# Turning the normed rows on VectorE and carrying the blocks with 32-partition copies, in a Fourier-mixing and feed-forward kernel

## The chip, the cores and the metric

The kernel runs on one core of a Trainium2 chip. The metric is device time in microseconds (us) of one execution: the median of several runs. Next to it stands one execution recorded by the hardware profiler. Engines are named as the profile names them: PE (TensorE; PEld is its weight load), DVE (VectorE), ACT (ScalarE), POOL (GpSimd), SP (SyncE). "L1195" is line 1195 of the kernel before.

## The reference, cut to what matters

```python
q_s = softmax(q, axis=-1); k_s = softmax(k, axis=2)      # B, H, S, DH = 8, 8, 576, 64
x   = q_s @ (k_s.T @ v)                                  # to (B, S, 512)
mixed = real(fft(fft(x, axis=1), axis=2))
u   = x + mixed
un  = (u - mean(u)) / sqrt(var(u) + 1e-6)
out = u + maximum(un @ w_ch1, 0.0) @ w_ch2               # 512 x 2048, 2048 x 512
```

All is computed in float32.

## The kernel before, in words

The 8 x 576 = 4608 rows of u are handled in nine groups of 512 rows: groups 0 to 7 hold 512 rows of one batch each, and group 8 the rows left over from all batches ("shared"). They are taken in the order 0, 1, ..., 6, 8, 7. Each group of four 128-row tiles passes an up stage (un times w_ch1, then relu) and a down stage (times w_ch2, plus u). Tile i has column half c = i % 2 of the group and row half u = i // 2. From the second group on, the up stage is a Strassen scheme of seven products (`ORDER = (1, 6, 5, 7, 2, 4, 3)`) in each of four pairs, L1334; from the third on, the down stage ("deep down") first runs product 1 (L1431), then three units of two products each, (2, 4), (7, 6) and (5, 3), in which the same scheme is applied once more (L1461).

While one group passes its stages, the next batch is prepared beside it: attention (with exponentials on ACT, L774 among them), the folded Fourier transform (`folded`, then `block`, L1087 and L1090, five of them, then `mix_own` and `mix_shared`, L1115 on), and the norm of the next group. `norm` takes the statistics of u (DVE, L1165), the root and scales (ACT L1169, DVE L1172), the normed tile un (ACT, L1189), turns it with four PE transposes of 128x128 into a PSUM tile (L1195), and copies that to the group's tile `unT` (ACT, L1204). `unT` is 128 x 7 x 2 x 256: seven slots, of which 0 to 3 hold the four quarters of un transposed and 4, 5, 1 and 6 get differences of quarters (`combine`: DVE and POOL, L1210; `combine_last`, L1215). The up stage's first products need slots 0, 5, 4 and 1, in this order. There is one buffer for `unT`, and the deep down stage of the group before uses its slots 0 to 5 as scratch in its unit (2, 4) only.

The order of work on each engine is written out by hand. Every step has a time in units ("steps") and an action; all steps are sorted by time, and each engine executes its instructions in that order, waiting at the head of its queue where data are late. In the deep down stage one unit is one product of eight matmul records on PE; the stage starts at 0, unit (2, 4) at 8, (7, 6) at 22, (5, 3) at 36, and the next up stage starts at 50. In a unit that starts at t the seven products start at t, t+2, ..., t+12. Their results are accumulated in three PSUM banks: ba (products 1 and 2), bb (6, 7, 4) and bc (5, 3). Between them other engines read the banks (`ends`): ACT copies ba after product 1 (L1475, at t+1.5) and after 2 (L1482, t+9.5); DVE reads bb after 6 (L1468, t+3.5) and after 7 (t+7.5, with one read of bc), bb after 4 (t+11.5) and bc after 3 (t+13.5). The next product into a bank waits for the read before it. On DVE and POOL there are also `a_step` (L1407: sums of blocks for the next unit; for (5, 3) at 25.3 to 32.4), and on POOL `into` and `sums` (L1411, L1414; additions to u and between blocks; from group 8's pass on both are done by DVE).

`norm` stands at step 29 of the down stage: statistics from 29.7, root 36.2, scales 38, normed tiles 38.3 to 42.2, transposes 40.8 to 44.7, copies 41.6 to 45.5, `combine` 46.5, `combine_last` 56.5. The norm of group 7 stands at step 14 of group 8's pass. In the first Strassen pass (group 1, "order 1"; its down stage has 56 steps without deep units, L1550) it stands at 29 too.

Of the kernel before, what the change touches and what calls it, by code (L numbers as in the profile page):

```python
# [40 lines left out]
F32 = mybir.dt.float32  # L41
# [5 lines left out]
P = 128  # L47
B, H, S, DH = 8, 8, 576, 64
D = H * DH
# [3 lines left out]
HD = D // 2  # L53
# [5 lines left out]
Q = 32  # L59
W = 2 * Q  # L60
NT = Q // 2 + 1
KT = D // P
VD = 4 * NC - S // Q
NF = FF // P
GT = 4 * P
NP = NF // 2

# [14 lines left out]
UP, TWICE = NP * len(ORDER), 8 + 6 * len(ORDER)  # L82
PAIRS = [(j + NP // 2, j) for j in range(NP // 2)]

DOWN = [(i, f) for n in range(4) for i in (2, 3, 0) for f in range(4 * n, 4 * n + 4)] + [(1, f) for f in range(NF)]
WARM = (3, 3), (24.7, 6), (41.9, 2), (43.45, 1), (44.5, 1)
# [32 lines left out]
def at(t, script):  # L119
    return [(t + dt, step) for dt, step in script]  # L120
# [17 lines left out]
class _Block:  # L138
    def __init__(self, ctx, tc, q, kT, v, w1, w2, ft, cd, out):
# [63 lines left out]

        self.big = c.tile([P, 3 * NF * D], F32, name="big")
        self.fifth = self.big[:, 3 * NF * D - 5 * P:3 * NF * D - P].rearrange("p (r n) -> p r n", n=P)
        nc.gpsimd.memset(self.fifth[0:64], 0.0)
        part = lambda i: self.big[:, i * NF * D:(i + 1) * NF * D].rearrange("p (f n) -> p f n", n=D)
        self.w1sb, self.w2sb, self.h0 = part(0), part(1), part(2)
# [15 lines left out]
    def turned(self):  # L224
        t = self.ps.tile([P, 4, P], F32, tag="tr", name="tr", bufs=2)
        return t
# [20 lines left out]
    def loads_first(self, fetch):  # L247

        nc, b = self.nc, 0
        at = 2 * NF * D  # L250

# [390 lines left out]
    def values_to(self, b, h):  # L642

        def load(i):
            first = VD * (i == 3)
            a = min(i * NC, S // Q - NC) + first
            v = self.v[b, :, h * HD:(h + 1) * HD].rearrange("(c s) n -> s c n", s=Q)[:, a:a + NC - first]
            self.nc.sync.dma_start(self.vt[i * Q:i * Q + Q, first:, 1:1 + HD], v)
# [3 lines left out]
    def prepare(self):  # L652
# [6 lines left out]
        for col in (0, 2 * P + 1):  # L659
            G.memset(self.vt[:, :, col:col + 1], 1.0)  # L660
        G.memset(self.vt[3 * Q:, 0:VD, :], 0.0)

# [493 lines left out]
    def norm(self, g):  # L1156

        nc, V = self.nc, self.nc.vector
        mv = self.small.tile([P, 4, 2], F32, tag="mv", name="mv", bufs=2)
        std = self.small.tile([P, 4], F32, tag="std", name="std", bufs=2)  # L1160
        uns, box = {}, {}

        def stats(i):
            st = self.small.tile([P, 6], F32, tag="st", name="st", bufs=2)
            V.bn_stats(st[:], self.xpart(g, i % 2, i // 2))  # L1165
            V.bn_aggr(mv[:, i, :], st[:])

        def root(s):
            nc.scalar.activation(std[:, s], mv[:, s, 1], ACT.Sqrt, bias=self.eps[:, 0:1])  # L1169

        def scales(s):
            V.reciprocal(std[:, s], std[:, s])  # L1172
            V.scalar_tensor_tensor(out=mv[:, s, 0], in0=mv[:, s, 0], scalar=-1.0, in1=std[:, s], op0=ALU.mult,
                                   op1=ALU.mult)

        def back():
            if g > 0:

                t = self.small.tile([P, 1], F32, tag="root", name="root", bufs=1)
                nc.scalar.activation(t[:], std[:, 0:1], ACT.Exp, scale=0.0)  # L1180

        def normal(i):
            un = self.halves()
            x = self.xpart(g, i % 2, i // 2)
            if g == 0 and i < 2:
                V.tensor_scalar(out=un[:, 0:D], in0=x, scalar1=std[:, i:i + 1], scalar2=mv[:, i, 0:1], op0=ALU.mult,
                                op1=ALU.add)
            else:
                nc.scalar.activation(un[:, 0:D], x, ACT.Identity, bias=mv[:, i, 0:1], scale=std[:, i:i + 1])  # L1189
            uns[i] = un  # L1190

        def turn(i):
            pt = self.turned()
            for k in range(KT):
                nc.tensor.transpose(pt[:, k, :], uns[i][:, k * P:(k + 1) * P], self.ident[:])  # L1195
            box[i] = pt

        def laid(i):
            if g not in self.unT:
                self.unT[g] = self.work.tile([P, 7, 2, HD], F32, tag="unT", name="unT", bufs=1)  # L1200
            c, u = i % 2, i // 2
            cols = slice(c * P, (c + 1) * P)
            copy = V.tensor_copy if g == 0 and c == u else nc.scalar.copy
            copy(self.unT[g][:, u:u + 3:2, :, cols], box.pop(i)[:].rearrange("p (a k) t -> p a k t", a=2))  # L1204

        def combine():
            if g > 0:
                some = lambda i: self.unT[g][:, i]
                for e, to, x, y in ((V, 4, 1, 0), (nc.gpsimd, 1, 3, 1), (V, 5, 3, 4)):
                    e.tensor_tensor(out=some(to), in0=some(x), in1=some(y), op=ALU.subtract)  # L1210

        def combine_last():
            if g > 0:
                some = lambda i: self.unT[g][:, i]
                V.tensor_tensor(out=some(6), in0=some(2), in1=some(5), op=ALU.subtract)  # L1215

        steps = []
        put = lambda t, f, *a: steps.append((t, lambda: f(*a)))
        if g == 0:
            for some in ((0, 2), (1, 3)):  # L1220
                s = slice(some[0], 4, 2)
                for i in some:
                    put(0, stats, i)
                for f in (root, scales):
                    put(0, f, s)
        else:
            for n, i in enumerate((0, 2, 1, 3)):
                put((0.7, 2.7, 4.7, 6)[n], stats, i)
            s = slice(0, 4)
            put(7.2, root, s)  # L1230
            put(9, scales, s)
            put(13.6, back)
        for n, i in enumerate((0, 2, 1, 3)):
            put(9.3 + 1.3 * n, normal, i)
            put(11.8 + 1.3 * n, turn, i)
            put(12.6 + 1.3 * n, laid, i)
        put(17.5, combine)
        put(27.5, combine_last)
        return steps
# [384 lines left out]
def kernel(ctx: ExitStack, tc: tile.TileContext, q, kT, v, w1, w2, ft,  # L1624
                                                           cd, out):
    blk = _Block(ctx, tc, q, kT, v, w1, w2, ft, cd, out)

    def timed(t, order, g):
        b = order + 1
        steps = at(t, blk.up(order, g)) + at(t + UP, blk.down(g, order))  # L1630
        if order == B:
            return steps + [(t + 6 + 1.2 * i, lambda i=i: blk.later and blk.later.pop(0)()) for i in range(36)]
        if b == B:
            return steps + at(t + UP + 14, blk.norm(groups[b]))
        start, end = -7 if order > 2 else 0, 45
        if b + 1 < B:
            steps += at(t, blk.ahead(b + 1))
        steps += at(t, blk.attention_timed(b, start, end)) + at(t + end, blk.folded(b))
        t += UP
        for i, k in enumerate((2, 3, 0, 1, 4)):  # L1640
            steps += at(t + 2 + 2 * i, blk.block(b, k))
        mixes = [blk.mix_own(b, c) for c in range(2)]
        if b % 2:
            mixes.insert(0 if b == B - 1 else 2, blk.mix_shared(b // 2))
        for i, some in enumerate(mixes):
            steps += at(t + 12.5 + 3.2 * i, some)
        return steps + at(t + 29, blk.norm(groups[b]))

    fetch, convert = blk.weights()

# [26 lines left out]
    groups = [*range(B - 1), B, B - 1]  # L1677
    first, second, both = 46.9, 56, 77
    steps = blk.opening(fetch, converted)
# [3 lines left out]
    t = first + second  # L1683
# [28 lines left out]
    t = 0  # L1712
    for order, g in enumerate(groups[1:], 1):
        later += timed(t, order, g)
        t += UP + (TWICE if order > 1 else UP)
# [59 lines left out]
```

## Time and profile before

| | |
|---|---|
| median of 3 runs | 1049.63 us (1049.01 to 1050.84) |
| profiled execution, its own time | 1050.86 us |
| its span, first to last instruction | 1049.1 us |
| PE clock granted | 0.998 |
| PE busy | 1034.9 us (99%) |
| DVE, ACT, POOL busy | 719.7, 456.3, 406.0 us |
| DMA | 236 MB, 225 GB/s on average |

Busy times are sums over one execution. PE's matmuls are pipelined, so their records overlap, and what a matmul costs is read from the starts of neighbours. The `unT` of group 2 is made at about 280 us, of groups 3, 4, 5, 6 and 8 at about 400, 511, 623, 734 and 847 us, and of group 7 at about 928 us (starts of the transposes).

### The profile page before, as it was taken

To read this page: it belongs to the slowest core of one execution; us is meant where nothing else is said; L and a number is where in the kernel's file an instruction comes from. 1 tells how busy PE (TensorE), PEld (TensorE's weight loads), DVE (VectorE), ACT (ScalarE), POOL (GpSimd) and SP (SyncE) were. 2 spreads that over 40 slices of the span, in tenths; PEclk is the share of its full clock that TensorE was granted. 3 is DMA by queue.
4 is the path that set the end of the run, shared out by engine and by line. 5 is a ranking of instruction groups with operands and counts; after the bars stand their busy time and mean duration, and the time that the engine had idled before them with its cause. 6 is when DMAs were issued, how large, how long until landed. Compare 5 with 4: busy or idle time off the path is not lost.

```text
span 1049.1 us, 16781 instructions
## 1 busy us (share of the span) xinstructions
PE 1034.9 (99%) x6178; PEld 901.0 (86%) x6178; DVE 719.7 (69%) x1410; ACT 456.3 (43%) x1141; POOL 406.0 (39%) x350
## 2 busy tenths in 40 slices
PE   8999999999999999999999999999999999999998
PEld 7844554888888899889998999989998998999898
DVE  5898888775476866777675777587658644774563
ACT  5674532862239216841475237822682132131210
POOL 3164420366333744555536544474346440000000
PEclk9999999999999999999999999999999999999999
DMA  8887598587999666955786567747644664576464
GB/s 254 258 266 257 172 255 285 185 243 231 290 321 231 214 219 245 238 201 193 259 225 201 201 241 242 217 176 256 228 154 178 224 241 161 216 255 221 171 224 147
DMA packets 114313, 236.01 MB, mean 225 GB/s; under 512 B 23272, under 2 KB 78696, under 8 KB 103608
## 3 DMA queue, kind: packets, MB, share of 16 engines
q1 hardware_dynamic: 113864, 234.42, 68.3%
q8 instruction: 49, 0.80, 0.3%
q14 instruction: 32, 0.26, 0.1%
q10 hardware_dynamic: 288, 0.26, 0.1%
q0 software_dynamic: 80, 0.26, 0.1%
HBM read 199.79 MB, written 39.06 MB: 228 GB/s over the span
## 4 chain that ended last, share of the span: by engine, by line
PE 81%; DVE 5%; DMA 3%; ACT 1%; issue 0%; POOL 0%; SPq 0%; DVEq 0%; ACTq 0%
PE bb L1334 15%; PE ba L1334 10%; PE bb L1461 10%; PE bc L1334 10%; PE bc L1461 7%; PE ba L1461 7%; PE bb L1431 5%; PE acc L715 2%; PE bb L1550 2%; PE acc L790 2%; DMA big<-w1s 2%; PE acc L1087 1%; PE acc L1090 1%; PE bc L1550 1%; PE ba L1550 1%; PE tr L1195 1%
## 5 line engine op out<-in xcount | busy, mean ns | idle before, releaser
L1334 PE MATMUL bb<-unT,big 128*128 128x256 f32 x768 | 182.0, 379 | 0.0
L1334 PEld LDWEIGHTS bb<-unT,big 128*128 128x128 f32 x768 | 144.3, 190 | 19.4 <-DVE u L1304 0.5
L1346 ACT ACTIVATE big<-big 128x512 f32<-128x512 f32 x96 | 60.3, 629 | 156.7 <-DVE big L1345 155.8
L1334 PE MATMUL ba<-unT,big 128*128 128x256 f32 x512 | 124.1, 379 | 1.1 <-DMA big<-w1s 1.1
L774 ACT ACTIVATE qT<-q 32x128 f32<-32x128 f32 x384 | 117.9, 307 | 13.9 <-DVE q L764 8.9
L1334 PE MATMUL bc<-unT,big 128*128 128x256 f32 x512 | 121.7, 379 | 0.0
L1334 PEld LDWEIGHTS bc<-unT,big 128*128 128x128 f32 x512 | 96.1, 190 | 13.2 <-DVE big L1345 0.7
L1334 PEld LDWEIGHTS ba<-unT,big 128*128 128x128 f32 x512 | 94.5, 190 | 13.3 <-DMA big<-w1s 1.3
L1461 PE MATMUL bb<-big 128*128 128x128 f32 x848 | 105.1, 275 | 0.3 <-DVE u L1468 0.3
L1304 DVE TENSOR_TENSOR u<-bb,s 128x512 f32<-128x512 f32 x66 | 45.4, 689 | 86.0 <-PE bb L1334 71.5
L1461 PEld LDWEIGHTS bb<-big 128*128 128x128 f32 x848 | 99.6, 192 | 0.5 <-DVE u L1468 0.5
L1411 POOL TENSOR_TENSOR x<-x,big 128x512 f32<-128x512 f32 x45 | 57.7, 1296 | 64.3 <-DVE big L1468 31.2
L1461 PE MATMUL ba<-big 128*128 128x128 f32 x640 | 79.6, 275 | 0.0
L1461 PEld LDWEIGHTS ba<-big 128*128 128x128 f32 x640 | 76.3, 192 | 1.2
L1407 DVE TENSOR_TENSOR big<-big 128x512 f32<-128x512 f32 x98 | 74.2, 796 | 0.0
L761 POOL TENSOR_TENSOR q<-q,qm 128x512 f32<-128x512 f32 x24 | 25.8, 1074 | 105.0 <-DVE qm L756 50.6
L1468 DVE TENSOR_TENSOR u<-bb,s 128x256 f32<-128x256 f32 x40 | 16.8, 421 | 67.6 <-PE bb L1461 63.3
L1210 POOL TENSOR_TENSOR unT<-unT 128x512 f32<-128x512 f32 x8 | 14.1, 1760 | 123.4 <-DVE unT L1210 123.4
L1431 PE MATMUL bb<-big 128*128 128x256 f32 x256 | 58.7, 380 | 0.0
L1345 DVE TENSOR_TENSOR big<-bc,u 128x512 f32<-128x512 f32 x64 | 44.0, 687 | 19.6 <-PE bc L1334 18.6
L384 POOL TENSOR_TENSOR big<-big 128x512 f32<-128x512 f32 x24 | 30.5, 1269 | 69.5 <-ACT big L1346 69.5
L1431 PEld LDWEIGHTS bb<-big 128*128 128x128 f32 x256 | 48.3, 190 | 7.8 <-DVE big L1345 0.8
(279 smaller groups left out, 2032.0 us busy)
## 6 DMA issues: line engine op xcount, KB each, us to landing
big<-w2d SPq DMA_DIRECT2D x67, 1024.0 KB
big<-w1s SPq DMA_DIRECT2D x64, 896.0 KB
big<-w2s SPq DMA_DIRECT2D x16, 1024.0 KB
big<-in_w_dram SPq DMA_DIRECT2D x21, 512.0 KB
w2d<-big SPq DMA_DIRECT2D x42, 256.0 KB
kb<-in_kT_dram SPq DMA_DIRECT2D x24, 320.0 KB
q<-in_q_dram SPq DMA_DIRECT2D x28, 256.0 KB
vt<-in_v_dram SPq DMA_DIRECT2D x36, 160.0 KB
```

The source lines that it names most:

```text
L384: e1.tensor_tensor(out=to(4), in0=at(2), in1=at(3), op=ALU.add)
L761: G.tensor_tensor(out=heads(), in0=heads(), in1=m[:].unsqueeze(2).to_broadcast([P, H, DH]), op=ALU.add)
L774: nc.scalar.activation(to[t, i * Q:i * Q + Q], one, ACT.Exp)
L1304: plus = lambda t: V.tensor_tensor(out=temp(t), in0=box["bb"][:], in1=box["s1"][:], op=ALU.add)
L1334: nc.tensor.matmul(bank()[:, i, :], lhsT=w[:, WA_AT[m], k * P:(k + 1) * P], rhs=self.unT[g][:, B_AT[m], k, :], start=first and i == 0 and ...
L1345: steps = [(0, lambda: V.tensor_tensor(out=hp(i), in0=bank()[:], in1=u()[:], op=ALU.add)), (0.8, lambda: nc.scalar.activation(hp(i), hp(i) ...
L1346: (0.8, lambda: nc.scalar.activation(hp(i), hp(i), ACT.Relu))]
L1407: e.tensor_tensor(out=to(o), in0=to(x), in1=to(y), op=op)
L1411: E.tensor_tensor(out=x, in0=x, in1=tile(m), op=ALU.add)
L1431: nc.tensor.matmul(box[name][:, i, :], lhsT=h[p][:, A_AT[m], i * P:(i + 1) * P], rhs=self.stream[n][:, p, :], start=p == 0 and (m != 1 or ...
L1461: nc.tensor.matmul(box[place[n]][:, i, :], lhsT=own(m)(A_AT[n])[:, f, :], rhs=w[:, r // 2, r % 2 * P:r % 2 * P + P], start=first and f == ...
L1550: nc.tensor.matmul(bank()[:, i, :], lhsT=h[p][:, A_AT[m], i * P:(i + 1) * P], rhs=w[:, p, :], start=first and i == 0 and p == 0, stop=p == ...
```

## The change

For groups 2 to 8 (`g > 1`) the norm gets an order of its own. It works in two halves, c = 0 and c = 1, of two tiles each. For each half: statistics at 0 and 1 (from the half's start), root 2, scales 3.2, normed tiles 4.2 and 5.2, then `turned` at 5.5 and 6.5: DVE transposes the 32x32 blocks of both tiles into one scratch, which is slots 4 and 5 of the same `unT` for either half. From 7.2 to 12.2 sixteen copies (`moved`) carry 32 partitions x 256 elements each from the scratch to their partitions and slots: eleven on ACT, five on POOL. The second half starts 7.5 steps after the first. Then follow `back` (at 14.1), `combine` (21.0) and `combine_last` (31.0). The PE transposes and the PSUM copies remain for groups 0 and 1.

The norm starts at step 25 instead of 29 (28.3 in order 1; group 7's stays at 14). In the deep passes the five blocks are placed at 0, 1.7, ..., 6.8 instead of 2, 4, ..., 10, and the mixes start at 11 instead of 12.5; in order 1 the blocks stay and the mixes start at 14.3.

```diff
+BY_POOL = (2, 5, 8, 11, 14)
...
+        def turned(i):
+            c, u = i % 2, i // 2
+            if g not in self.unT:
+                self.unT[g] = self.work.tile([P, 7, 2, HD], F32, tag="unT", name="unT", bufs=1)
+            box[c] = self.unT[g][:, 4:6].rearrange("p a k n -> p (a k n)")
+            of = uns[i][:, 0:D].rearrange("p (a k t q) -> p t a k q", a=2, k=2, t=4)
+            V.transpose(box[c].rearrange("p (t a u k q) -> p u t a k q", t=4, a=2, u=2, k=2)[:, u], of)
+
+        def moved(c, j, t):
+            rows = slice(j * Q, (j + 1) * Q)
+            of = box[c][rows, t * 2 * P:(t + 1) * 2 * P].rearrange("s (n q) -> s n q", q=Q)
+            a = c * P + j * Q
+            to = self.unT[g][t * Q:(t + 1) * Q, 0:4, :, a:a + Q].rearrange("s i k q -> s (i k) q")
+            copy = nc.gpsimd.tensor_copy if 4 * j + t in BY_POOL else nc.scalar.copy
+            copy(to, of)
...
+        if g > 1:
+            for c in range(2):
+                t = 7.5 * c
+                for n, i in enumerate((c, c + 2)):
+                    put(t + n, stats, i)
+                    put(t + 4.2 + n, normal, i)
+                    put(t + 5.5 + n, turned, i)
+                put(t + 2, root, slice(c, 4, 2))
+                put(t + 3.2, scales, slice(c, 4, 2))
+                for n in range(16):
+                    put(t + 7.2 + .33 * n, moved, c, n // 4, n % 4)
+            put(7.5 + 6.6, back)
+            put(7.5 + 8.2 + 16 * .33, combine)
+            put(7.5 + 18.2 + 16 * .33, combine_last)
+            return steps
...
-        t += UP
+        t, soon = t + UP, 2 * (order == 1)
         for i, k in enumerate((2, 3, 0, 1, 4)):
-            steps += at(t + 2 + 2 * i, blk.block(b, k))
+            steps += at(t + soon + (1.7 if order > 1 else 2) * i, blk.block(b, k))
...
-            steps += at(t + 12.5 + 3.2 * i, some)
-        return steps + at(t + 29, blk.norm(groups[b]))
+            steps += at(t + 11 + 1.65 * soon + 3.2 * i, some)
+        return steps + at(t + 25 + 1.65 * soon, blk.norm(groups[b]))
```

## The prediction

> **What bounds the kernel now.** I read the page's busy times first, then the cores (one core, granted clock 0.998), then the groups by form, then the timelines of PE, DVE, ACT and POOL around one transition.
>
> ```profile
> PE 1034.9 (99%) x6178; PEld 901.0 (86%) x6178; DVE 719.7 (69%) x1410; ACT 456.3 (43%) x1141; POOL 406.0 (39%) x350
> ```
>
> PE is the bound: only an instruction that PE no longer issues, or a wait that it newly gets, moves the time. These are the prices that the sum needs (the form of the groups is: count | busy us, mean ns | idle before):
>
> ```profile
> L1195 PE MATMUL tr<-ident,eo 128*128 128x128 f32 x144 | 21.4, 274 | 1.8 <-ACT eo L1189 1.3 <-ACT unT L1204 0.5
> L764 DVE STREAM_TRANSPOSE q<-q 128x512 f32<-128x512 f32 x24 | 17.0, 707 | 6.2 <-POOL q L761 5.8
> L774 ACT ACTIVATE qT<-q 32x128 f32<-32x128 f32 x384 | 117.9, 307 | 13.9 <-DVE q L764 8.9
> L1346 ACT ACTIVATE big<-big 128x512 f32<-128x512 f32 x96 | 60.3, 629 | 156.7 <-DVE big L1345 155.8
> L952 POOL TENSOR_TENSOR F<-T 128x256 f32<-128x256 f32 x4 | 2.6, 656 | 10.0 <-DVE F L953 10.0
> L169 POOL MEMSET Zr<- 128x256 f32 x1 | 0.3, 302 | 0.0
> ```
>
> And the place, PE's timeline where group 4 is normed during group 3's down pass:
>
> ```profile
> 510.19 1.06 PE L1461 MATMUL bc<-big 128*128 128x128 f32 x8
> 511.08 0.60 PE L1195 MATMUL tr<-ident,eo 128*128 128x128 f32 x4
> 511.52 1.06 PE L1461 MATMUL bc<-big 128*128 128x128 f32 x8
> 512.41 1.06 PE L1461 MATMUL bb<-big 128*128 128x128 f32 x8
> ...
> 519.08 1.95 PE L1461 MATMUL bc<-big 128*128 128x128 f32 x16
> 520.87 1.89 PE L1334 MATMUL ba<-unT,big 128*128 128x256 f32 x8
> ```
>
> PE never stands still here. Four transposes move it by 511.52 - 511.08 = 0.44 us; their 274 ns each are mostly pipeline. DVE and ACT at the same place:
>
> ```profile
> 496.40 1.75 DVE L1407 TENSOR_TENSOR big<-big 128x512 f32<-128x512 f32 x1
> 498.08 0.41 DVE L1468 TENSOR_TENSOR u<-bb,s 128x256 f32<-128x256 f32 x1
> 498.41 3.55 DVE L1407 TENSOR_TENSOR big<-big 128x512 f32<-128x512 f32 x4
> ...
> 510.46 0.42 DVE L1468 TENSOR_TENSOR u<-bb,s 128x256 f32<-128x256 f32 x1 [2.65 <-ACT eo L1189]
> ```
>
> ```profile
> 508.93 2.23 ACT L1189 ACTIVATE eo<-x,mv,std 128x512 f32<-128x512 f32 x3
> ```
>
> DVE has no gap from 494.65 to 507.8, and its L1407, 0.60 us when alone (1.89 for three at 928.53), takes up to 1.75 beside a POOL operation. The L1468 at 510.46 matters most: it reads bank bb between two products that use it, and PE's next product into bb starts at 512.41.
>
> **What goes.** Seven groups lose 16 transposes: 7 x 4 x 0.44 = 12.3 us of PE, 1.77 a group. At them PE waited almost never (1.8 us over all nine groups, 1.3 of it one wait), so no stall goes with them. ACT loses four evacuations of 0.58. The Trainium skill, TensorE: Matmul & The Clock Gate, Part 4, puts a transpose in a kernel at about 275 ns; with that as PE's price the gain would be 112 x 0.275 = 31 us, but it is the record's length, which the trace has as 274, and not the advance of 0.11.
>
> **What comes, per group.** Four DVE transposes of 128x512: L764 has 0.71 (the next operation 0.63 later), and its durations beside POOL operations stay 0.70 to 0.71; L708, whose write is strided too, is no dearer per element, so 0.63 each. Twenty-two ACT copies of 32x256: no such row. Below is L774, 32x128 in 0.307, starting every 0.319 (ten in 3.19 from 444.81); above L1346, 128x512 in 0.629. By elements between them: 0.307 + 128 x 0.322/384 = 0.41, and 0.42 from start to start, since L774 and L678 (32x16, 0.20, four in 0.84) start only after the one before. Ten POOL copies: between the memset (0.30) and the two-input L952 (0.66), I take 0.5. The table loads stay two (1.28 each), since nothing between root and back needs another table. So ACT gets 22 x 0.42 - 2.3 = 6.9 us a group and DVE 2.5; both have room on average, and what counts is their order.
>
> **The path, group 4, on the clock of before.** PE's order there is unchanged but for the transposes, so it would want its fourth product (bank bb) at 512.41 - 0.44 = 511.97. For that DVE must have read bb, and L1468's step (39.5) now stands behind the turns of the second half (38 and 39). Those wait for the second half's normals and for all sixteen copies of the first half, because both halves use the same scratch, slots 4 and 5 of unT.
> - DVE up to the second turn (steps 25 to 31.5): two halves of statistics 1.64, six L1407 3.6, three L1468 1.1, scales 0.4, two turns 1.3: 8.0. The six L1407 took 5.96 here instead of 3.6 because of POOL, whose operations remain: 10.3. It starts when the additions of the mixes end, at 496.4 before; they come 1.5 steps earlier, one step being 1.79/2 = 0.89 us of PE, but behind work that does not move, so 495.8. The second turn ends at 506.1.
> - ACT then: eleven copies 4.6, the second root 0.3, two normals 1.5, L1475 0.3, in one queue: 512.9.
> - DVE: last turn 0.7, then L1468 0.4: 514.05, PE goes on at 514.15.
>
> PE stands 2.2 us where it saved 1.77: 0.45 lost. Next is the start of the up pass, now at 521.3. ACT: table load and back 1.4, eleven copies 4.6, from 512.9 to 518.9; POOL from 513.65 with two 1.27 additions between its copies: 2.5 + 2.5 = 518.7; the two combinations on DVE 1.4: 520.4. Slot 5 is wanted at 523.0, so this is covered by 2.6 us. The keys' maxima and exponentials behind it slip by about 0.6 and have 1.7 (first L708 ends 524.34, its PE user starts 526.05).
>
> **The other edits.** The blocks come earlier: PE reaches the third about 5.4 us after the down pass starts (467.49), while DVE's last L1055 for it ends at 473.12, 5.6 after. That is a new PE wait of 0.25, but it is time in which DVE and ACT run on, so it comes off the 2.2 and adds nothing. If the chain above is hidden, it costs 4 x 0.25 (group 3 has 0.6 to spare). The mixes' move costs nothing: their consumers on DVE are in the queue just summed. Neither move can gain by itself, since PE did not wait there. The order-1 pass (group 2) has 6.9 us per product, and DVE's reads of banks there have one product of room; its combination waits behind an L1369 that a DMA holds to 289 anyway, and slot 5 is ready about 293.7 for 295.8. Group 2 gains its 1.77.
>
> Group 7 (beside group 8's pass) starts at step 14. The first turn now waits until PE has read slot 5 of the old tile (924.5, the end of L1461 at 922.56). Second turn with an L1407 between: 926.4. Five copies, L1475, root, scales, L1407 and L1468: 930.6, where PE wants bb at 929.70: 1.0. Then six copies and two normals to 933.3, turn, three DVE additions of 0.6 and the next L1468: 936.1, for a product wanted at 934.3: 1.9. Together 2.9; the POOL copies can hold DVE's additions for 0.5 more, as the 1.75 row shows: 3.4 against 1.77, 1.6 lost.
>
> **Sum.** Five groups 5 x 0.45 = +2.25, group 7 +1.6, group 2 -1.77: +2.1 us. The profiled execution took 1050.86 (span 1049.1 and 1.8 around it), 1.2 above the median of the runs. It becomes 1053.0; against the median, 1049.63 + 2.1 = 1051.7.
>
> **Rivals.**
> - *Shorter copies.* The L1346 at 465.64 takes 0.63, yet the next instruction, L1341, starts at 466.18: ACT overlaps there. If the small copies overlap by the same 0.1, eleven are 1.1 us shorter: the five groups lose 1.1 and gain 1.77 (+0.65 each), group 7 is about 0.7 better. 1049.63 - 3.3 + 0.9 - 1.8 = 1045.5. Against it: L774 and L678 don't overlap. It decides below about 0.38 from start to start. The Trainium skill, ScalarE: Activation LUTs, What ACT_TABLE_LOAD costs, says that back-to-back ACTIVATEs overlap by about 93 ns; by that and its 186 ns + 0.833 ns an element a copy is an estimated 0.31 and this rival holds. L774's 0.319 for a record of 0.307 speaks against it, L1189's three in 2.23 (0.71 apart, 0.81 long) for it where partitions stay.
> - *No wait at all.* If DVE ran 2.2 us earlier than I have it, or the read of bb were ahead of the turns: 1049.63 - 12.3 = 1037.3. DVE's unbroken 13 us and the order of steps speak against it.
> - *The copies are longer.* At 0.53, towards the 0.629 row, the chain is 1.2 longer: five groups lose 1.65, group 7 2.8: +8.2 + 2.8 - 1.8, 1058.9. From 0.65 (or 1.05 on POOL) the up pass also waits for slot 5. It decides above 0.46. For it: the write goes in runs of 32 elements, and POOL copies lock against DVE's additions.
>
> **Chances.** No wait 0.06, shorter copies 0.16, forecast 0.53, longer copies 0.25. A difference under 0.2% (2.1 us) can hardly be told from none. The forecast lies on that border, its own range being 1048.5 to 1056 (half a microsecond a group in the start of DVE's queue), so its share falls about evenly: same 0.25, slower 0.28 and, with the longer copies, 0.53; faster 0.22. The range, 1043 to 1060, leaves out the case without a wait and the far ends of two rivals.
>
> **What would show it.** Transposes at L1195 fall from 144 to 32. The ACT copies start every 0.42. PE gets a wait of about 2 us in each of five groups, before the fourth product of the last unit of the down pass, released by DVE's L1468 after a turn; in group 7 two, before products 7 and 4 of the unit (7, 6). The up pass does not wait for unT. I am wrong if PE waits less than 1.5 us in those places, if it waits at the up pass, or if group 2's stage gets a wait of its own.

## The result and the profile after

The changed kernel takes 1061.2 us (median of 4 runs, 1060.25 to 1063.17); the kernel before, run beside it, takes 1049.32. The ratio is 1.0113 with an interval of 1.0094 to 1.0133: slower by over 0.2%, by 11.9 us where +2.1 was forecast, and outside the range. The profiled execution took 1061.91, its span is 1060.1 us, 11.0 longer than before (10.4 up to PE's last product, 0.6 behind it).

The page of the changed kernel, busy times:

```profile
PE 1027.7 (97%) x6066; PEld 889.5 (84%) x6066; DVE 739.5 (70%) x1452; ACT 507.2 (48%) x1274; POOL 430.9 (41%) x420
```

PE issues 112 instructions fewer and is busy 7.2 us less, yet the span grew: the loss is, in the main, time in which PE stands. The new groups (line engine op, form, count | busy us, mean ns of one | idle time before):

```profile
L1221 ACT COPY unT<-unT 32x256 f32<-32x256 f32 x154 | 61.9, 402 | 19.3 <-DVE unT L1213 17.6
L1221 POOL COPY unT<-unT 32x256 f32<-32x256 f32 x70 | 29.5, 421 | 100.8 <-DVE unT L1213 98.2
L1213 DVE STREAM_TRANSPOSE unT<-eo 128x512 f32<-128x512 f32 x28 | 19.2, 700 | 17.7 <-ACT unT L1221 12.6 <-ACT eo L1190 2.4 <-PE bc L1493 1.4
```

The prices came out as forecast: 402 ns a copy on ACT, 421 on POOL, 700 a turn on DVE. What stands beside the turns matters more: they waited 12.6 us in all for copies. (New line numbers: the bank reads of the deep pass, L1468 before, are L1500; its products L1493, the up products L1366, DVE's bank reads there L1336 and L1377, the ACT copies out of ba L1507 and L1514, the keys' turns L709, the combinations L1227.) PE's waits in the changed kernel, those that are new (total us, times, longest):

```profile
PE bb L1493 <- DVE u L1500: 13.0, 11, 2.7
PE bb L1366 <- DVE u L1336: 2.3, 4, 0.6
```

Before, the second row was not there, and the first stood at 0.3 us, once:

```profile
PE bb L1461 <- DVE u L1468: 0.3, 1, 0.3
```

Both name DVE reading bank bb. PE's timeline around the same transition as in the prediction (start, us, the idle time before it and its releaser in brackets):

```profile
510.68 1.95 PE L1493 MATMUL bc<-big 128*128 128x128 f32 x16
514.08 2.05 PE L1493 MATMUL bb<-big 128*128 128x128 f32 x16 [1.44 <-DVE u L1500]
...
521.32 1.89 PE L1366 MATMUL ba<-unT,big 128*128 128x256 f32 x8
...
528.35 1.97 PE L1366 MATMUL bb<-unT,big 128*128 128x256 f32 x8 [0.56 <-DVE u L1336]
```

and DVE and ACT at that place:

```profile
511.83 0.71 DVE L1213 STREAM_TRANSPOSE unT<-eo 128x512 f32<-128x512 f32 x1 [2.21 <-ACT unT L1221]
513.00 0.71 DVE L1213 STREAM_TRANSPOSE unT<-eo 128x512 f32<-128x512 f32 x1 [0.46 <-ACT eo L1190]
513.63 0.39 DVE L1500 TENSOR_TENSOR u<-bb,s 128x256 f32<-128x256 f32 x1
...
519.14 2.19 DVE L1227 TENSOR_TENSOR unT<-unT 128x512 f32<-128x512 f32 x2
...
526.78 0.84 DVE L709 STREAM_TRANSPOSE kb<-kb 128x640 f32<-128x640 f32 x1 [0.91 <-ACT kb L700]
527.55 0.65 DVE L1336 TENSOR_TENSOR u<-bb,s 128x512 f32<-128x512 f32 x1
```

```profile
506.02 2.06 ACT L1221 COPY unT<-unT 32x256 f32<-32x256 f32 x5 [2.31 <-DVE unT L1213]
...
514.39 4.53 ACT L1221 COPY unT<-unT 32x256 f32<-32x256 f32 x11
```

In the order of time: the third turn waits 2.21 us for the first half's copies, the fourth for a normed tile; only then does DVE take L1500, for which PE has stood 1.44. Later DVE queues its read L1336 behind the second turn of the keys; that turn waits for ACT's exponentials, and PE stands a second time, in the up pass. Eleven copies in 4.53 us are 0.412 each.

In the pass beside which group 7 is normed, the same wait is the longest, and something follows it:

```profile
943.70 2.87 PE L1493 MATMUL bb<-big 128*128 128x128 f32 x16 [2.68 <-DVE u L1500]
946.37 2.80 PE L1493 MATMUL bc<-big 128*128 128x128 f32 x16
```

Sixteen products take 2.8 us where 1.95 is usual. The table by stretch shows why (the column after POOL is the granted PE clock, 1 being full speed):

```profile
core 0: us, PE busy (x) PEld busy (x) DVE busy (x) ACT busy (x) POOL busy (x), PEclk, DMA share, GB/s
943.00:946.00 3.00, 2.30 (x15) 2.30 (x16) 2.97 (x6) 2.88 (x9) 1.88 (x3) 0.79 0.67 279
946.00:949.00 3.00, 3.00 (x19) 3.00 (x19) 2.34 (x5) 0.32 (x1) 1.27 (x1) 0.64 0.44 111
```

The clock fell to 0.5 from 944.73 for 3.41 us.

Where the time went is read from the starts of the passes on PE (first matmul of each), as the change of each pass' length against before, in us:

| pass | changed kernel |
|---|---|
| start to the first pass | -0.46 |
| beside group 2's norm | -1.75 |
| up pass after the norm of 2 | +0.47 |
| up passes after the norms of 3, 4, 5, 6 | +1.00, +0.81, +1.00, +0.80 = +3.6 |
| deep passes beside the norms of 3, 4, 5, 6, 8 | +0.50, +0.70, +0.86, +0.70, +1.76 = +4.5 |
| deep pass beside group 7's norm | +4.02 |
| all others | 0.0 |
| sum at the last pass' end | +10.4 |

The first row and the up pass after group 2's norm vary from run to run: in that pass PE waits for a DMA of weights (1.1 us before, 1.5 here, none in some of the runs below), and its difference goes from -1.22 to +0.98 over the kernels below. Not all of that is the DMA: in two of them (group 7 as before, +0.98; all copies on ACT, +0.81) PE also stands 0.8 in that pass for work of DVE, which the changed kernel's own trace does not show.

### The profile page after: what moved, and what is told of

It reads as the page before. It is cut to its first block, busy times and chain, and to the rows that moved or that the text cites. A ratio compares the mean times of both kernels' runs of the same rounds, so it can differ in the third digit from the quotient of the medians.

```text
span 1060.1 us, 16833 instructions
## 1 busy us (share of the span) xinstructions
PE 1027.7 (97%) x6066; PEld 889.5 (84%) x6066; DVE 739.5 (70%) x1452; ACT 507.2 (48%) x1274; POOL 430.9 (41%) x420
## 4 chain that ended last, share of the span: by engine, by line
PE 64%; DVE 15%; ACT 6%; DMA 3%; issue 2%; POOL 0%; SPq 0%; ACTq 0%; DVEq 0%
PE bb L1366 14%; PE ba L1366 9%; PE bc L1366 9%; PE bb L1493 6%; PE bb L1463 5%; PE ba L1493 3%; PE bc L1493 3%; DVE big L1439 3%; ACT unT L1221 2%; PE bb L1582 2%; PE acc L791 2%; PE acc L716 2%; DMA big<-w1s 2%; PE acc L1088 1%; PE acc L1091 1%
## 5 line engine op out<-in xcount | busy, mean ns | idle before, releaser
L1366 PE MATMUL bb<-unT,big 128*128 128x256 f32 x768 | 182.3, 380 | 2.3 <-DVE u L1336 2.3
L1366 PEld LDWEIGHTS bb<-unT,big 128*128 128x128 f32 x768 | 144.2, 190 | 22.4 <-POOL x L1443 2.9
L1366 PE MATMUL ba<-unT,big 128*128 128x256 f32 x512 | 124.1, 379 | 1.5 <-DMA big<-w1s 1.5
L1366 PE MATMUL bc<-unT,big 128*128 128x256 f32 x512 | 121.8, 379 | 0.0
L1493 PE MATMUL bb<-big 128*128 128x128 f32 x848 | 106.3, 278 | 13.2 <-DVE u L1500 13.0
L1493 PEld LDWEIGHTS bb<-big 128*128 128x128 f32 x848 | 100.0, 193 | 15.7 <-DVE u L1500 15.7
L1366 PEld LDWEIGHTS bc<-unT,big 128*128 128x128 f32 x512 | 96.1, 190 | 13.3 <-DVE big L1377 0.7
L1366 PEld LDWEIGHTS ba<-unT,big 128*128 128x128 f32 x512 | 94.5, 190 | 13.7 <-DMA big<-w1s 1.7
L1336 DVE TENSOR_TENSOR u<-bb,s 128x512 f32<-128x512 f32 x66 | 45.4, 688 | 83.5 <-PE bb L1366 71.4
L1443 POOL TENSOR_TENSOR x<-x,big 128x512 f32<-128x512 f32 x45 | 58.3, 1305 | 69.0 <-DVE big L1500 25.3
L1493 PE MATMUL ba<-big 128*128 128x128 f32 x640 | 78.0, 275 | 0.0
L1493 PEld LDWEIGHTS ba<-big 128*128 128x128 f32 x640 | 75.2, 192 | 0.7
L1221 ACT COPY unT<-unT 32x256 f32<-32x256 f32 x154 | 61.9, 402 | 19.3 <-DVE unT L1213 17.6
L1221 POOL COPY unT<-unT 32x256 f32<-32x256 f32 x70 | 29.5, 421 | 100.8 <-DVE unT L1213 98.2
L762 POOL TENSOR_TENSOR q<-q,qm 128x512 f32<-128x512 f32 x24 | 25.0, 1042 | 104.7 <-DVE qm L757 46.3
L1377 DVE TENSOR_TENSOR big<-bc,u 128x512 f32<-128x512 f32 x64 | 44.0, 687 | 19.4 <-PE bc L1366 18.6
```

Source lines behind the costliest of these rows:

```text
L762: G.tensor_tensor(out=heads(), in0=heads(), in1=m[:].unsqueeze(2).to_broadcast([P, H, DH]), op=ALU.add)
L1221: copy(to, of)
L1336: plus = lambda t: V.tensor_tensor(out=temp(t), in0=box["bb"][:], in1=box["s1"][:], op=ALU.add)
L1366: nc.tensor.matmul(bank()[:, i, :], lhsT=w[:, WA_AT[m], k * P:(k + 1) * P], rhs=self.unT[g][:, B_AT[m], k, :], start=first and i == 0 and ...
L1377: steps = [(0, lambda: V.tensor_tensor(out=hp(i), in0=bank()[:], in1=u()[:], op=ALU.add)), (0.8, lambda: nc.scalar.activation(hp(i), hp(i) ...
L1443: E.tensor_tensor(out=x, in0=x, in1=tile(m), op=ALU.add)
```

## The experiments

Three theories were set against each other. *Queue*: DVE's reads of PSUM banks stand, in DVE's order, behind turns, combinations and key turns that wait for the copies; PE stands because those reads come late. *Places*: the moved blocks and mixes cost the time. *Lock*: POOL's copies and DVE hinder each other, and the time is lost to that.

**Blocks and mixes at their old places, turns kept.**

```diff
-        t, soon = t + UP, 2 * (order == 1)
+        t, soon = t + UP, 2
...
-            steps += at(t + soon + (1.7 if order > 1 else 2) * i, blk.block(b, k))
+            steps += at(t + soon + 2 * i, blk.block(b, k))
...
-            steps += at(t + 11 + 1.65 * soon + 3.2 * i, some)
-        return steps + at(t + 25 + 1.65 * soon, blk.norm(groups[b]))
+            steps += at(t + 12.5 + 3.2 * i, some)
+        return steps + at(t + (25 if order > 1 else 28.3), blk.norm(groups[b]))
```

> The changed kernel with the blocks and mixes back at their places of before; the norm keeps its new order and start. Theory Queue (DVE's reads of PSUM banks stand in its queue behind the turns, which wait for ACT's copies and normals): the 0.28 us wait at the third block goes from four passes (-1.1 us), but the mixes' additions, and with them the statistics and turns, come 1.3 us later, so the wait before product 7 of unit (5, 3) grows by up to 1.3 in five passes: 1061 to 1067 us. Theory Places (it is the earlier blocks and mixes that cost, by their own waits and by what they push on DVE): 1050 to 1054 us.

Measured: 1060.54 us, ratio 1.011 (1.0075 to 1.0146). The waits for L1500 grew from 13.0 to 16.3 us, and two of the deep passes lost 1.85 and 1.84 in place of 0.50 and 0.86 (the five together 6.7 in place of 4.5); group 7's pass lost 2.39 in place of 4.02, since the clock did not fall there in this execution. The time lies 0.5 under Queue's range and 6.5 above that of Places: the old places do not help, and PE's waits for the reads are longer with them.

**The moves alone, turns as before.**

```diff
-        if g > 1:
+        if g > 9:
...
-        return steps + at(t + 25 + 1.65 * soon, blk.norm(groups[b]))
+        return steps + at(t + 29, blk.norm(groups[b]))
```

> The kernel before with only the blocks and mixes moved as in the change; norm, its start and its PE transposes as before. Queue: only the wait at the third block, 4 x 0.28, is new: 1049.5 to 1051.5 us. Places: most of the loss is there already, some 10 us above what the transposes would give back, 1055 to 1062 us.

Measured: 1050.24 us, ratio 1.0014 (0.9999 to 1.0029), and no wait for L1500 among PE's waits. Places falls.

**The second half's turns behind the bank read.** Only the order on DVE is changed.

```diff
-                    put(t + 5.5 + n, turned, i)
+                    put(t + (7.1 + .05 * n if c else 5.5 + n), turned, i)
```

> The changed kernel with the two turns of the second half (steps 38 and 39) put behind DVE's read of bank bb (step 39.5), nothing else. Queue: DVE stood idle for 2.2 us before the first of these turns in the trace, so the turns come no later, and the wait of 1.6 us before product 7 of unit (5, 3) goes in five passes: 8 us less there. The up pass then starts 1.6 earlier while its inputs and the keys' exponentials come when they came, so part of it returns there: 1054 to 1058 us. A POOL lock as the cause (Lock) would leave it at 1061 us, and so would Places.

Measured: 1055.37 us, ratio 1.006 (1.0043 to 1.0077). Four of the five deep passes now beat before by 0.53 to 0.73 and group 7's loses 1.16 in place of 4.02, but the up passes lose 2.3 to 2.5 each in place of 0.8 to 1.0. PE's waits in this kernel:

```profile
PE bb L1366 <- DVE big L1500: 4.7, 4, 1.2
PE bb L1493 <- DVE u L1500: 4.5, 6, 1.4
```

The second row shrank from 13.0 to 4.5, and the first is new: the turns are later, so the copies and the combination are later, and the next bank read stands behind the combination. DVE's timeline of this kernel at that place:

```profile
516.51 2.39 DVE L1227 TENSOR_TENSOR unT<-unT 128x512 f32<-128x512 f32 x2 [1.24 <-ACT unT L1221]
...
519.98 0.41 DVE L1500 TENSOR_TENSOR big<-bb,s 128x256 f32<-128x256 f32 x1
```

The wait moved to the next read in the queue, as Queue says; it is not removed while the chain behind the turns is as long.

**The copies taken out.** The 16 copies of a half are replaced by one ACT copy of 128x1024 that leaves out the carrying to other partitions.

```diff
+        def carried(c):
+            to = self.unT[g][:, 0:4, :, c * P:(c + 1) * P].rearrange("p i k q -> p (i k) q")
+            nc.scalar.copy(to, box[c].rearrange("p (n q) -> p n q", q=P))
...
-                for n in range(16):
-                    put(t + 7.2 + .33 * n, moved, c, n // 4, n % 4)
+                put(t + 7.2, carried, c)
```

> The changed kernel with the sixteen copies of each half replaced by one ACT copy of 128 partitions x 1024 elements, which leaves out the carrying to other partitions (blocks stay in their partitions). Queue: ACT's part of the chain shrinks from 4.6 to about 1 us per half, the turns of the second half come 3 us earlier, and all waits of PE before product 7 and in the up pass go; the transposes' 12.3 us come in but for the 1.1 at the blocks and something in group 7, where the first turn still waits for PE: 1038 to 1042 us. Places: 1055 or more. Lock: also about 1040, since no copy is on POOL.

Measured: 1044.31 us, ratio 0.9958 (0.9944 to 0.9972). With the chain short, the change gains. The deep passes gain 1.08, 1.01, 0.71 and 0.86 (group 8's loses 0.19), the up passes lose at most 0.28, group 7's pass gains 0.24. It stays 2 us and more above the 1038 to 1042 that Queue gave: the copies are not the whole of it. In group 4's pass, where 1.77 was removed, the starts on PE show two stops left, 0.36 at the third block (with the restart after it) and 0.39 before a product of the unit (7, 6): 1.77 - 0.75 = 1.02, the measured gain. The first comes from the blocks' new place, the second from a read of DVE (L1503 in this kernel) behind sums that POOL slows; neither has to do with a copy.

**Group 7 as before, the rest changed.**

```diff
-        if g > 1:
+        if g > 1 and g != 7:
```

> The change with one group left out of it: group 7 is normalised as before, with 16 PE transposes and no copies; groups 2 to 6 and 8 keep the new turns. In the changed kernel's marks the pass of group 7's norm is 4.02 us longer than before, with PE waits of 0.93 and 2.68 and then 3.41 us at a granted clock of 0.5. Theory Queue (DVE's bank reads stand behind the turns and combines, which wait for the copies): both waits go, the clock stays at 1, the pass comes back to before's length within 0.3, and the time is about 1057.2 (1061.2 minus 4.0). Theory Clock (the fall of the clock is a thing of its own, and not the wait's): the waits' 2.3 us go, the fall stays in this or another place, about 1059. Other passes as in the changed kernel: up passes of groups 4 to 8 +0.5 to +1.0 each, deep passes +0.5 to +0.9.

Measured: 1056.83 us, ratio 1.0064 (1.0041 to 1.0087). That pass is back to +0.00 and the clock stays at 1 there: the fall belongs to the wait.

**One bank read ahead of the second key turn.**

```diff
-            for dt, f in ((8.3, turn), (12.3, times), (14, scale)):
+            for dt, f in ((8.3 + .3 * (r == 1 and start < 0), turn), (12.3, times), (14, scale)):
```

> The change with one instruction moved on DVE's queue: the second turn of the keys (L709) is queued behind DVE's read of the first bank of the up product (L1336) and no longer ahead of it; all other engines keep their order. Theory Queue: PE's wait of 0.56 to 0.6 for L1336, four times, goes; the up passes lose 0.6 to 0.8 of their +0.47 to +1.0 each, in all 2.4 to 3.2, so about 1058.4; deep passes as in the changed kernel. If the key turn itself is what is late (its users on PE wait for it), the wait moves to the key products and the time stays within 0.7 of 1061.2.

Measured: 1057.3 us, ratio 1.0075 (1.0054 to 1.0095), 3.9 below the changed kernel. In the profiled executions the passes differ by 4.4. Of that, 1.6 is group 7's pass, where PE waited 2.69 as in the changed kernel but the clock did not fall, 0.8 the up pass with the DMA and 0.55 the start; only the rest is the moved read. The up passes after the norms of 3 to 6 fell from +1.00, +0.81, +1.00, +0.80 to +0.42, +0.55, +0.41, +0.55, by 1.7 in all where 2.4 to 3.2 was expected: the read's place was worth 0.25 to 0.6 a pass. What is left is DVE's queue still being late: in two of these passes for the queries, which PE now waits for, and in the other two for a read L1336 again (0.28 each).

```profile
421.97 0.63 PE L913 MATMUL tr<-ident,q 128*128 128x128 f32 x4 [0.44 <-DVE q L885]
```

**All copies on ACT.**

```diff
-BY_POOL = (2, 5, 8, 11, 14)
+BY_POOL = ()
```

> The change with all 32 copies of a group on ACT and none on POOL: a half's chain is 16 x 0.41 = 6.6 us on ACT and no longer 11 x 0.41 = 4.5. Theory Queue (the chain of copies ahead of DVE's next read sets the waits): each half ends 2.1 us later; PE's waits for the bank reads grow by about 2 us per group in the five deep passes and by up to 2 in group 7's: 1061.2 + 6 x 2 = about 1073, 1067 at the least; DVE's combine gets shorter (1.4 and not 2.2 for two instructions), which gives back 0.8 a group at the most. Theory Lock (POOL and DVE hinder each other, and that is what the time was lost to): no POOL copies, so the time falls below 1059.

Measured: 1080.5 us, ratio 1.0296 (1.0271 to 1.0322): worse than Queue's 1073. The wait before product 4 is 3.5 us in every pass, 2.1 longer than with eleven copies, as five copies more of 0.412 make it. The excess is the clock, which now falls in the five deep passes:

```profile
518.92 3.35 PE L1493 MATMUL bb<-big 128*128 128x128 f32 x16 [3.52 <-DVE u L1500]
```

As the main cause Lock falls with it: with no POOL copy the two combinations are shorter (691 ns each over the run, 939 in the changed kernel), and the kernel is slower. That POOL's own sums slow DVE's, and so make reads later, holds all the same (2.38 for two sums, below).

**The copies shared 8 to 8.**

```diff
-BY_POOL = (2, 5, 8, 11, 14)
+BY_POOL = (1, 3, 5, 7, 9, 11, 13, 15)
```

> The change with the 16 copies of a half shared 8 to 8 between ACT and POOL, and not 11 to 5. On ACT the first half's chain is 8 x 0.41 = 3.3 us in place of 4.5, and POOL needs 8 x 0.42 = 3.4. Theory Queue: the second half's turns start about 1.2 earlier, so PE's wait of 1.44 before the bank read falls to about 0.3 (-1.1 in each of five deep passes) and group 7's 2.68 to 1.5, too short for the fall of the clock (-2.9): -8.4. Against it, POOL's second eight copies stand among its sums into x (five copies and three sums ended at 520.04 in group 4's norm); three more copies put its last copy at about 520.5, and the combine, which began at 519.14, 1 to 1.5 later: up passes +0.6 to +1.5, five times, +3 to +7. Together 1061.2 - 8.4 + 5 = about 1058, between 1055.5 and 1060. If only the number of copies on ACT counted, it would be 1052.8; if POOL's copies hold DVE up, above 1061.

Measured: 1055.84 us, ratio 1.0072 (1.0057 to 1.0088). The wait before product 4 in group 4's pass fell from 1.44 to 0.39, group 7's pass from +4.02 to +1.15, and the up passes rose to +1.9 to +2.1 each:

```profile
PE bb L1493 <- DVE u L1500: 6.5, 11, 1.6
PE bb L1366 <- DVE big L1500: 3.0, 4, 0.8
```

As the third experiment did by order, this one trades a wait in the deep pass for one in the up pass, here through POOL, whose copies stand among its own sums.

**Half of it: the first half turned by DVE, the second by PE.** Eight PE transposes a group go, and the scratch is used once.

```diff
-                    put(t + 5.5 + n, turned, i)
+                    if c == 0:
+                        put(t + 5.5 + n, turned, i)
+                    else:
+                        put(t + 10.1 + 1.4 * n, turn, i)
+                        put(t + 10.9 + 1.4 * n, laid, i)
...
-                for n in range(16):
+                for n in range(16 * (c == 0)):
...
-            return steps + at(t + UP + 14, blk.norm(groups[b]))
+            return steps + at(t + UP + 16.2, blk.norm(groups[b]))
...
-            steps += at(t + soon + (1.7 if order > 1 else 2) * i, blk.block(b, k))
+            steps += at(t + soon + ((0, 1.7, 4.1, 5.2, 6.8)[i] if order > 1 else 2 * i), blk.block(b, k))
```

> The change for one half of each group alone: the first half of groups 2 to 8 is turned by DVE and carried by 16 copies, the second half by 8 PE transposes as before, at its old distance; the third block is put 0.7 later, so that its first product does not stand ahead of DVE's read of the bank, and group 7's norm 2.2 later. Removed from PE: 7 x 2 x 0.44 = 6.2 us. Theory Queue: the first half's copies end before the second half's scaling needs ACT, no turn and no combine waits for a copy in front of a bank read, and the time is 1049.3 - 6.2 = 1043.1 plus waits of 0 to 0.5 a group: 1043 to 1047. If the carrying itself costs, wherever it lies (ACT's time, POOL's port), half of the changed kernel's loss remains: (12 + 12.3)/2 = 12 us against the 6.2 gained, so 1055.

Measured: 1048.8 us, ratio 0.9994 (0.9982 to 1.0006): no difference, where Queue gave 1043 to 1047 and a cost of the carrying itself 1055; both missed. The passes of groups 2 and 7 gained their 0.87, and no up pass lost time. The deep passes of 3 to 6 stood at -0.16 to +0.06, group 8's at +0.88. Beside group 3's norm 0.88 was gained and 0.95 lost, in two stops before products into bb. The first on DVE:

```profile
387.57 2.38 DVE L1443 TENSOR_TENSOR big<-big 128x512 f32<-128x512 f32 x2
389.87 0.41 DVE L1504 TENSOR_TENSOR u<-bb,s 128x256 f32<-128x256 f32 x1
```

Two sums stand ahead of the read (L1504 in this kernel, L1443 the sums), and beside POOL they take 2.38 us. The second on ACT, whose copy out of ba (L1511), which another read needs, stands behind the eleventh small copy:

```profile
398.28 0.40 ACT L1221 COPY unT<-unT 32x256 f32<-32x256 f32 x1
398.71 0.37 ACT L1511 COPY s<-ba 128x256 f32<-128x256 f32 x1
```

**The same, with these two orders changed.**

```diff
-                    put(t + 7.2 + .33 * n, moved, c, n // 4, n % 4)
+                    put(t + 7.2 + .33 * n + 2.6 * (n > 8), moved, c, n // 4, n % 4)
...
-                put(t + 2 * k + 1.5, ends, unit, o)
+                put(t + 2 * k + 1.5 - .3 * (i == 2 and k in (1, 3)), ends, unit, o)
```

> The half-and-half kernel with two orders changed. (a) On ACT, copies 10 to 16 of the first half are queued behind the copy of a product out of its bank that opens the unit (5,3) (L1511), and no longer ahead of it. (b) On DVE, the two bank reads of the unit (7,6) that let PE go on with products 5 and 2 are queued ahead of the sum L1443 that stood right before them. In the half-and-half kernel each deep pass lost 0.88 us of gain to two PE waits, of 0.52 (DVE's L1504 at 389.87 behind two L1443 of 2.38) and 0.33 (L1504 at 399.11 behind ACT's L1511 at 398.71, which stood behind 11 copies and a normalisation). Theory Queue: both waits go, each deep pass of groups 3 to 6 gains 0.8 to 0.9 and group 8's 1.5; 1048.8 - 4 x 0.85 - 1.5 = about 1044, at a ratio of 0.995. If the carrying costs by its length and not by its place, nothing of this moves and the time stays within 1 of 1048.8.

Measured: 1045.5 us, ratio 0.9968 (0.9956 to 0.998): faster than the kernel before by 3.0 us (1048.49, run beside it), where the changed kernel was slower than it by 11.9. The deep passes beside the norms of 3 to 6 now gain 0.49 to 0.56, and group 8's stands at -0.01. Its page has PE busy all through again:

```profile
PE 1029.7 (99%) x6122; PEld 894.7 (86%) x6122; DVE 727.5 (70%) x1438; ACT 484.4 (46%) x1211; POOL 413.1 (40%) x385
```

It is 1.5 short of the 1044 expected. Beside group 3's norm 0.38 of the first stop is left, since the one sum that still precedes the read takes 1.78 beside POOL:

```profile
387.99 1.78 DVE L1443 TENSOR_TENSOR big<-big 128x512 f32<-128x512 f32 x1
389.69 0.41 DVE L1504 TENSOR_TENSOR u<-bb,s 128x256 f32<-128x256 f32 x1
```

## Why the prediction was wrong

The terms that held:

- *What goes.* 1.77 a group: group 2's pass gained 1.75 (and 0.87 with half of the transposes). The record length of 275 ns, by which 31 us would have come off PE, is refuted: 112 transposes fewer took 7.2 us off its busy time and at most 1.75 off a pass.
- *Prices.* ACT's copy 0.41 and 0.42 from start to start (0.402 and 0.412), the turn 0.63 from start to start (513.00 to 513.63). POOL's copy was taken at 0.5 between 0.30 and 0.66 and is 0.421. So the rival of longer copies, whose 1058.9 lay nearest to the result, did not happen, and neither did that of shorter ones. The Trainium skill, ScalarE: Activation LUTs, What ACT_TABLE_LOAD costs, gives 186 + 0.833 x 256 = an estimated 399 ns for one such copy; the trace agrees (402). Its overlap of 93 ns between neighbours is not seen here: the starts are 412 apart.
- *The path for group 4.* Second turn predicted to end at 506.1 (505.93), ACT done at 512.9 (512.96), L1468 done at 514.05 (514.02), PE on at 514.15 (514.08), up pass at 521.3 (521.32). These times flatter the forecast: the changed kernel starts this pass 0.25 earlier than the kernel before (467.24 against 467.49), so on the clock of before each of them came 0.25 later. The forecast was 0.45 lost, the pass lost 0.70. And, as forecast, the up pass does not wait for `unT`.

The steps that failed, in order of their size:

1. *"The keys' maxima and exponentials behind it slip by about 0.6 and have 1.7", and the up pass as covered.* This term was 0 and measured +3.6 over four up passes. The step looked at the wrong consumer. I followed the first key turn to its user on PE; but DVE's queue goes on from the combination to the keys' maxima, their turns and then L1336, the read of a bank that PE wants soon after. The rows of before (L1210 is the combination, L1304 the read):

```profile
518.39 1.42 DVE L1210 TENSOR_TENSOR unT<-unT 128x512 f32<-128x512 f32 x2 [0.49 <-ACT unT L1204]
526.03 0.65 DVE L1304 TENSOR_TENSOR u<-bb,s 128x512 f32<-128x512 f32 x1
527.17 1.89 PE L1334 MATMUL bb<-unT,big 128*128 128x256 f32 x8
```

The slip of 0.6 was wrong too: the combination starts 0.75 later and takes 2.19 and not 1.42 where POOL works beside it, so that all behind it comes 1.52 later, the first key turn (525.02 for 523.50) and the read (527.55 for 526.03) alike. The up pass itself starts 0.45 later, which leaves 1.07. Before, PE went on 0.49 after the read's end, after the change 0.15 after it, so 0.34 was to spare: 1.07 - 0.34 = 0.73, and 0.08 for the restart, are the 0.81 that this pass lost. The run with that one read moved gave 1.7 of the 3.6 back.

2. *Group 7, 3.4 of waits against 1.77, 1.6 lost.* The waits were 0.93 and 2.68, so the chain was right to 0.2; but the pass lost 4.02. A stop costs more than its idle time: from one start to the next, with the slower restart after it (one start 0.213 after the other in place of 0.112), the two cost 1.19 and 2.94. The rest, 4.02 + 1.77 - 4.13 = 1.66, is the fall of the clock, sixteen starts 0.1 further apart. In the run with the read ahead of the key turn, where the clock stayed, the same two stops made the pass lose 2.41.
3. *"Five groups 5 x 0.45 = +2.25"*, measured +4.5. Group 4 was worked out at one read, and the others were taken to be alike. The passes beside groups 3, 4, 5 and 6 lost 0.50, 0.70, 0.86 and 0.70, 0.96 more in all than forecast. In each of the four an earlier read, in the unit (7, 6), is late as well, behind sums that POOL slows; it stops PE for 0.62, 0.39, 0.62 and 0.39 with the restart. Group 8's pass lost 1.76, 1.31 more. There the trace of before already has a stop of 0.52 with its restart (the wait of 0.3 above, from 834.42), so DVE was late before anything was added; after the change the third block and three reads are late in it, by 0.36, 0.64, 1.32 and 1.71 with their restarts: 4.03 - 0.52 - 1.75 = 1.76. For the block's wait, the step "it comes off the 2.2 and adds nothing" is nearly right: group 4's pass stops for 0.36, 0.39 and 1.71, 2.46 in all where 2.2 was forecast in one.

Added up, the sum lacked 3.6, 2.4 and 2.25 in these steps, and 0.47 in the up pass with the DMA: 2.1 + 3.6 + 2.4 + 2.25 + 0.47 - 0.46 = 10.4, the measured sum of passes.

Behind the first and the third step is one mistake: I checked one bank read of DVE's queue in one pass, and took those ahead of it and behind it as in time. Shown is that the later reads are hit in their turn (the read after the combination with the turns put back or the copies shared 8 to 8, L1336 with its own move), and that the length of ACT's chain sets the wait (five copies more, 2.1 us more; three fewer, 1.05 less). Two of the three signs that I had named for being wrong are there: PE "waits at the up pass", and the wait before the fourth product, 1.44, is "less than 1.5 us", since PE had already stood at earlier places of the pass. How much of the loss POOL's own sums make, by slowing those of DVE ahead of the reads, no run here takes apart.

## What to carry to other kernels

Where PE's banks are emptied by an engine that works in one order, list every bank read of that engine from the first moved instruction to a full stage behind the inserted chain, and for each the work in front of it that waits for the chain; checking one and calling the rest covered finds only part of the loss. Moving the turns or sharing the copies otherwise only changed which read is late; halving the chain and putting the reads ahead of what they do not need made the change pay. A transpose on PE costs its advance (0.11 us here), so 22 x 0.402 + 10 x 0.421 + 4 x 0.70 = 15.9 us of copying and turning a group, in exchange for 1.77 us of PE, must stand ahead of nothing that PE waits for.

## What the runs showed of the hardware

*The clock falls after a stop of under 3.4 us, by a fixed grid.* In the kernel with all copies on ACT the granted clock falls to 0.5 at 403.37, 519.42, 635.47, 751.53 and 870.99, each time for 3.413 us; the distances are 34, 34, 34 and 35 times 3.413. On that grid, the window that ended at a fall held 2.38 to 3.36 us of PE's idle time, while the stop of 957.85 to 961.30 (3.44 us long) was divided by the grid into 1.89 and 1.55, and no fall came. In the changed kernel the window that ended at 944.73 held 2.39 of the 2.68. The two other kernels with a stop of 2.7 us, blocks and mixes at their old places and the read ahead of the key turn, had no fall: their grids (marked by where each one's clock record starts) divided it into 1.82 and 0.85, and into 1.13 and 1.55. So a stop of 2.7 us cost 1.7 more in one of three profiled executions that had one, by where it fell on the grid; stops up to 1.76 never did. Between 1.9 and 2.4 us of idle time in a window no run here decides. The Trainium skill, TensorE: Matmul & The Clock Gate, Part 1, states a free-running window of 3413 ns, with which the grid agrees, and a fall after an idle window; here a window with about 0.7 of its time idle was enough.

*A sum on DVE can cost more beside a sum on POOL, a turn does not.* The sums L1443 above took 1.78 beside a POOL sum and 0.68 alone; the turns take 0.71 beside a POOL sum (two of them in the changed kernel, twelve with the copies shared 8 to 8) and 0.66 to 0.71 without one. No turn ran beside a POOL copy. POOL's one-input copy of 32x256 takes 0.421 in the changed kernel and 0.429 where it does half of the copies.
